# Weights, q, stores and low parts rearranged at the start of a fused attention and two-layer kernel

## The chip, the cores and the metric

The kernel runs on one core of a Trainium2 chip. The metric is the device time of one execution in microseconds (us); less is better. A core has TensorE (PE, matmuls), VectorE (DVE), ScalarE (ACT), GpSimd (POOL) and SyncE (SP), which here issues every DMA.

## The reference

Linear attention with an RMS norm, then two feed-forward layers, all in fp32:

```
kv  = einsum('bhsd,bhse->bhde', k, v)          # b=8, h=8, s=576, d=64
out = einsum('bhsd,bhde->bhse', q, kv)
out = out / sqrt(mean(out*out, -1) + 1e-6) * g_norm
x   = out, tokens x 512                        # 4608 x 512
x   = relu(x @ moe_w_in)**2 @ moe_w_out        # 512 -> 2048 -> 512
h   = x @ moe2_w_in;  x = (h * cos(h)) @ moe2_w_out
```

The layer weights arrive as 64-bit floats.

## The kernel before

A layer matmul is made of three fp32r matmuls on split operands: every fp32 value is a high part (a cast to fp32r, on ScalarE) plus a low part (a subtraction of the high part), and the product is high x high, high x low and low x high. So each weight (`wh`, `wl`), each x (`xh`, `xl`) and each activation (`gh`, `gl`) needs a cast and a subtraction before TensorE can use it.

`load_w` brings half of the weights of one f (128 of the 2048 inner columns) as raw 64-bit words, 512 KB, and `conv_w` turns them into `wh` and `wl`: five VectorE steps (L120, L122, L125, L128, L131), a ScalarE step (L121), the cast (L132) and the subtraction (L133, GpSimd). The raw tiles have two buffers; a `Stream` object loads item k+2 one chunk after item k is converted. There are 16 values of f, i = 0 is the w_in half and i = 1 the w_out half. Conversion k stands here for the k-th item: f = k // 2, i = k % 2.

The layer work is a list of chunks (stage, token tile t of 512 tokens, f). Stage 0 is the first layer with f = 0 to 7, stage 1 the same layer with f = 8 to 15, stage 2 the second layer with all 16. `layer_in` makes 12 matmuls of a chunk into a PSUM bank, `act_relu2` or `act_cos` makes `gh` and `gl`, and `layer_out` makes 12 matmuls into the accumulators, two chunks later. In stage 0, chunk n below 8 is f = n of the first token tile and needs conversion 2n for `layer_in` and 2n + 1 for `layer_out`.

Attention is cut in units (batch b, head pair group p of 4, half hf of 288 tokens). `load_kv` and `kv_mm` make K'V of a batch (five loads with five buffers), then for each unit `att_a` (matmul with q, square, scaled copy `og`), `att_b` (sum of squares by a matmul with ones, r and r2 on ScalarE), `att_c` (three VectorE operations, L251 to L253, into `xo`, and its store to `x_d`) and `att_d`, which for the first two token tiles (NDIRECT) writes `xh` and `xl` straight from `xo`. Later tiles fetch x from DRAM by `load_x` and split it by `split_x`.

Everything that isn't a chunk is a job with a position, in chunks: `at(n, fn, ...)`. Jobs run in the order of their positions between the chunks; all with n up to -1 come ahead of chunk 0. Batch 0 of the attention has its kv_mm at -13.5 and unit i at -13 + i (`att_b`, `att_c` and `att_d` at 1.5 more), batch 1 starts at -3 with steps of 0.8, and each later batch fills the eight chunks of one token tile. Weight conversions 0 to 15 stand at -5 + 0.7 k. On top of that the framework's scheduler works over the program: it orders each engine's instructions by readiness in its own plan, with the program order as priority. So an engine's order in the trace can differ from the order of positions (conversions 0 and 1 run ahead of the attention in the trace, although their positions are behind it).

The pool `att` is given back when the attention's chunks are over, and the second half of the weights is kept in its place.

Of the kernel before, what the change touches and what calls it, by code (L numbers as in the profile page):

```python
# [24 lines left out]
def kernel(  # L25
# [22 lines left out]
    NH = 8  # L48
    NW = NF // 2
    NEXACT = 2  # L50
    NQ = 4
    XH, XL = 8, 10
    S = NT // B
    HS = S // 2
# [45 lines left out]
    wpools = {0: wlo}  # L100

    def load_w(m, f, i):
        raw = conv_p.tile([P, DM, 2], U32, tag="raw", name="raw")
        nc.sync.dma_start(out=raw.rearrange("p n two -> p (n two)"), in_=(wA, wB)[m][f, :, i, :])
        raws[m, f, i] = raw

    def conv_w(m, f, i):
        raw = raws.pop((m, f, i))
        low, high = raw[:, :, 0], raw[:, :, 1]
        ahead = (m, f) in spooled  # L110
        if ahead:
            h, l = (tp.tile([P, DM], F32R, tag="t", name=f"w{x}")[:] for x in "hl")
        else:
            if i == 0:
                new_w(m, f)
            h, l = (x[:, i, :] for x in wts[m, f])
        e = tp.tile([P, DM], U32, tag="t", name="e")
        w = tp.tile([P, DM], U32, tag="t", name="w")
        ef, wf = e[:].bitcast(F32), w[:].bitcast(F32)
        nc.vector.tensor_scalar(out=e, in0=high, scalar1=0x7FF00000, scalar2=None, op0=ALU.bitwise_and)  # L120
        nc.scalar.activation(out=e[:].bitcast(I32), in_=e[:].bitcast(I32), func=AF.Relu, scale=8.0, bias=expb)  # L121
        nc.vector.tensor_scalar(  # L122
            out=w, in0=high, scalar1=12, scalar2=8, op0=ALU.logical_shift_left, op1=ALU.logical_shift_right
        )
        nc.vector.scalar_tensor_tensor(  # L125
            out=w, in0=low, scalar=28, in1=w, op0=ALU.logical_shift_right, op1=ALU.bitwise_or
        )
        nc.vector.scalar_tensor_tensor(  # L128
            out=e, in0=high, scalar=0x80000000, in1=e, op0=ALU.bitwise_and, op1=ALU.bitwise_or
        )  # L130
        nc.vector.scalar_tensor_tensor(out=wf, in0=w, scalar=float(1 << 24), in1=ef, op0=ALU.add, op1=ALU.mult)  # L131
        nc.scalar.copy(out=h, in_=wf)  # L132
        nc.gpsimd.tensor_tensor(out=l, in0=wf, in1=as32(h), op=ALU.subtract)  # L133
        if ahead:
            for k, x in enumerate((h, l)):
                nc.sync.dma_start(out=w_d[m, f][:, k, i, :], in_=as32(x))
# [77 lines left out]
    def att_a(*u):  # L214
        b, p, hf = u
        o = bank("o")[:, :HS]
        nc.tensor.matmul(o, kvs[b][:, p, :], q_sb.pop(u)[:], start=True, stop=True)  # L217
        og = att_p.tile([P, HS], F32, tag="og", name="og", bufs=4)
        sq = att_p.tile([P, HS], F32, tag="sq", name="sq", bufs=3)
        nc.scalar.activation(out=sq, in_=o, func=AF.Square)  # L220
        nc.scalar.activation(out=og, in_=o, func=AF.Copy, scale=gcol)
        if b < NEXACT:
            att[u] = (og, sq, None)
            return
        sh = att_p.tile([P, HS], F32R, tag="sh", name="sh", bufs=3)
        sl = att_p.tile([P, HS], F32R, tag="sl", name="sl", bufs=3)
        nc.scalar.copy(out=sh, in_=sq)
        nc.vector.tensor_tensor(out=sl, in0=sq, in1=as32(sh[:]), op=ALU.subtract)
        att[u] = (og, sh, sl)
# [15 lines left out]
    def att_c(*u):  # L245

        b, p, hf = u
        og, ss, r, r2 = att[u]
        m = att_p.tile([P, HS], F32, tag="m", name="m", bufs=2)
        xo = att_p.tile([P, HS], F32, tag="xo", name="xo", bufs=3)  # L250
        nc.vector.scalar_tensor_tensor(out=m, in0=ss, scalar=D * EPS, in1=r2, op0=ALU.add, op1=ALU.mult)  # L251
        nc.vector.scalar_tensor_tensor(out=m, in0=m, scalar=-3.0 * D, in1=r, op0=ALU.add, op1=ALU.mult)
        nc.vector.tensor_tensor(out=xo, in0=m, in1=og, op=ALU.mult)  # L253
        nc.sync.dma_start(out=x_d[b][:, p, hf * HS:(hf + 1) * HS], in_=xo)
        att[u] = xo

    def att_d(*u):
        b, p, hf = u
        xo = att.pop(u)
        tok = b * S + hf * HS  # L260
        for t in range(NDIRECT):
            lo, hi = max(tok, t * TOK), min(tok + HS, (t + 1) * TOK)
# [4 lines left out]
            h, l = (x[:, lo - t * TOK:hi - t * TOK] for x in xs[0, t, p])  # L267
            piece = xo[:, lo - tok:hi - tok]
            nc.scalar.copy(out=h, in_=piece)
            eng = nc.gpsimd if b == 0 else nc.vector  # L270
            eng.tensor_tensor(out=l, in0=piece, in1=as32(h), op=ALU.subtract)  # L271

    def units(b):
        return [(b, p, hf) for p in range(NKC) for hf in range(2)]
# [15 lines left out]
                n += 1  # L290
        return ps

    def act_relu2(ps, lo_eng, busy=False):
        r = tp.tile([P, TOK], F32, tag="t", name="r")
        g = tp.tile([P, TOK], F32, tag="t", name="g")
        h = g_p.tile([P, TOK], F32R, tag="gh", name="gh")
# [4 lines left out]
        else:  # L301
            nc.vector.scalar_tensor_tensor(out=g, in0=ps, scalar=0.0, in1=r, op0=ALU.max, op1=ALU.mult)
        nc.scalar.copy(out=h, in_=g)  # L303
        lo_eng.tensor_tensor(out=l, in0=g, in1=as32(h[:]), op=ALU.subtract)  # L304
        return h, l

    def act_cos(ps, lo_eng):
        k = tp.tile([P, TOK], I32, tag="t", name="k")
        y = tp.tile([P, TOK], F32, tag="t", name="y")
        h = g_p.tile([P, TOK], F32R, tag="gh", name="gh")  # L310
# [6 lines left out]
        nc.scalar.activation(out=c, in_=y, func=AF.Sin, bias=hpib)  # L317
        nc.vector.tensor_tensor(out=y, in0=ps, in1=c, op=ALU.mult)  # L318
        nc.scalar.copy(out=h, in_=y)  # L319
        lo_eng.tensor_tensor(out=l, in0=y, in1=as32(h[:]), op=ALU.subtract)  # L320
        return h, l

    def load_part(t):
# [61 lines left out]
    class Stream:  # L385
# [7 lines left out]
                self.load(*item)  # L393
            self.next += count

        def place(self, positions, after=0):
            for n, item in zip(positions, self.items):
                at(n, self.use, *item)
                at(n + after, self.advance)

    spooled = {(0, f) for f in range(NW, NF)} | {(1, f) for f in range(NH, NF)}
    conv_at = [
        (0, range(NH), -5, 0.7),
        (0, range(NH, NW), 4, 0.8),
        (0, range(NW, NF), 13, 2.6),
        (1, range(NH), nA0 + 5, 2.1),
        (1, range(NH, NF), nA0 + 5 + 2 * NH * 2.1, 2.1),
# [10 lines left out]
        w_items += [(m, f, i) for f in fs for i in range(2)]  # L418
        w_at += [n + step * k for k in range(2 * len(fs))]
    w_stream = Stream(load_w, conv_w, w_items)  # L420
    w_stream.place(w_at, 1)

    kv_stream = Stream(load_kv, kv_mm, [(b, c) for b in range(B) for c in range(NSC)])
    starts = [(-13, 1), (-3, 0.8)] + [(-3 + NH * (b - 1), NH / (2 * NKC)) for b in range(2, B)]
# [2 lines left out]
    for b, (s0, ds) in enumerate(starts):  # L427
        for i, u in enumerate(units(b)):
# [4 lines left out]
            q_items = q_items[1:]  # L433
            for fn in (att_b, att_c, att_d):
                at(n + 1.5, fn, *u)
    for st in range(3):
        f0 = NH if st == 1 else 0
        for t in range(NTILE):
            n0 = index[st, t, f0]
            for c in range(NKC):  # L440
                if st == 0 and t < NDIRECT:
                    continue
                at(n0 - 5 + c, load_x, st, t, c)
                at(n0 - 4 + c, split_x, st, t, c)
            if st == 1:
                at(n0 + 3, load_part, t)
    jobs.sort(key=lambda j: j[:2])
    done = 0

# [7 lines left out]
    def run_chunks(lo, hi, act):  # L457
        for n in range(lo, hi):
            ps = layer_in(*chunks[n])
            gs[chunks[n]] = act(ps, nc.gpsimd if n < 4 else nc.vector, *([True] if n < nAtt else []))  # L460
            run_jobs(n)
            if n >= LAG:
                layer_out(*chunks[n - LAG])
            run_jobs(n + 0.5)

    nc.vector.memset(epsb, EPS)
    nc.vector.memset(hpib, HALF_PI)
    nc.vector.memset(qrtb, 0.25)
    nc.vector.memset(expb, -float((896 + 24) << 23))
    nc.vector.memset(as32(ones[:]), 0.0)  # L470
    for j in range(2):
        nc.vector.memset(as32(ones[j * D:(j + 1) * D, j * D:(j + 1) * D]), 1.0)

    with tc.tile_pool(name="att", bufs=1) as att_p:
        kvx = [att_p.tile([P, NKC, P], F32, tag=f"kvx{b}", name=f"kvx{b}") for b in range(2)]
# [1 line left out]
            nc.gpsimd.memset(x, 0.0)  # L477
        w_stream.advance(2)
        kv_stream.advance(NSC)
        for u in units(0)[:NQ]:  # L480
            load_q(*u)
        for j in range(2):
            nc.sync.dma_start(out=gcol[j * D:(j + 1) * D, :], in_=g_norm.rearrange("(d o) -> d o", o=1))
        nc.vector.tensor_scalar(out=gcol, in0=gcol, scalar1=-0.5 / D, scalar2=None, op0=ALU.mult)
        run_jobs(-1)
        banks.update(o=["o"], ss=["ss"])
        run_chunks(0, nAtt, act_relu2)
# [48 lines left out]
```

## Time and profile before

| | us |
|---|---|
| median of 3 runs | 1717.36 (1714.54 to 1719.39) |
| profiled execution | 1713.82 |
| its span (first to last instruction) | 1712.0 |
| TensorE busy | 1677.3 (98%) |
| VectorE busy | 1000.1 (58%) |
| ScalarE busy | 774.5 (45%) |
| GpSimd busy | 245.2 (14%) |

Of the 40 equal slices of the span (42.8 us each) TensorE is busy 6, 7 and 9 tenths in the first three or nine and more in all others but the last. Busy times are sums of durations; an instruction's duration can overlap the start of the next on the same engine, and a matmul's end is modelled. Lines named L120 and so on are those of the program above. In rows, "PEld" is TensorE's weight load, "SPq" a DMA issue on SP, "<-" after the numbers names what ended the idle time before an instruction, and the granted clock of TensorE is given as a share of full speed. A row of stretches holds the stretch and its length, the busy us (and number of instructions) of PE, PEld, DVE, ACT and POOL, the granted clock, the share of the DMA engines and GB/s.

### The profile page before, as it was taken

How to read it: one execution, taken by the hardware profiler on the slowest of the kernel's cores; microseconds unless marked ns; L12 is line 12 of the kernel's file. 1: busy time of each engine (PE TensorE's matmuls, PEld its weight loads, DVE VectorE, ACT ScalarE, POOL GpSimd, SP SyncE). 2: the span in 40 equal slices, each digit the busy share in tenths (PEclk: the TensorE clock that was granted, in tenths of full speed). 3: DMA queues.
4: the chain of work that ended last, by engine and by line, in shares of the span. 5: the costliest groups of instructions: out<-in, count | busy, mean ns of one | idle time of the engine just before them, and what ended most of it. 6: DMA issues, size and time to landing. Idle time of an engine off the chain costs nothing.

```text
span 1712.0 us, 20153 instructions
## 1 busy us (share of the span) xinstructions
PE 1677.3 (98%) x7488; PEld 1381.6 (81%) x7488; DVE 1000.1 (58%) x1561; ACT 774.5 (45%) x1366; POOL 245.2 (14%) x186
## 2 busy tenths in 40 slices
PE   6799999999999999999999999999999999999998
PEld 5488888888888888878888888888888888888887
DVE  5974666566223555555555565656565656565655
ACT  5665666667333333333334343434343434343333
POOL 2321112112111222222221010101010101010000
PEclk9899999999999999999999999999999999999999
DMA  8554646544712333345457010101010101000000
GB/s 256 176 186 149 208 156 203 175 138 146 255 50 74 123 123 123 120 151 169 151 165 278 1 49 1 49 1 50 1 50 1 50 1 47 3 31 13 6 20 25
DMA packets 81571, 170.15 MB, mean 99 GB/s; under 512 B 10560, under 2 KB 38720, under 8 KB 81472
## 3 DMA queue, kind: packets, MB, share of 16 engines
q1 hardware_dynamic: 81472, 168.86, 30.3%
q8 instruction: 59, 0.97, 0.2%
q14 instruction: 40, 0.33, 0.1%
HBM read 114.30 MB, written 54.53 MB: 99 GB/s over the span
## 4 chain that ended last, share of the span: by engine, by line
PE 91%; DVE 3%; DMA 1%; issue 1%; ACT 1%; POOL 0%; SPq 0%; DVEq 0%; ACTq 0%; POOLq 0%
PE acc L343 44%; PE l L289 25%; PE ss L289 9%; PE o L289 9%; PE o L217 1%; PE o L193 1%; DVE w L125 1%; DVE e L128 1%; DVE w L131 0%; PE ss L237 0%; DMA xraw<-x_d 0%; PE ss L238 0%; DVE w L122 0%; DVE e L120 0%; DMA xraw<-y_d 0%
## 5 line engine op out<-in xcount | busy, mean ns | idle before, releaser
L289 PE MATMUL l<-xh,wh 128*128 128x512 f32 x688 | 270.8, 394 | 6.7 <-ACT r L298 4.8
L289 PE MATMUL l<-xh,wl 128*128 128x512 f32 x688 | 270.1, 393 | 2.4 <-POOL wl L133 2.4
L171 POOL TENSOR_TENSOR xl<-xraw,xh 128x512 fp32r<-128x512 f32 x100 | 141.2, 1416 | 912.9 <-ACT xh L170 890.9
L289 PE MATMUL l<-xl,wh 128*128 128x512 f32 x688 | 270.6, 393 | 0.4 <-POOL xl L271 0.4
L343 PE MATMUL acc<-gh,wh 128*128 128x512 f32 x576 | 235.4, 409 | 1.4 <-DVE ev L361 1.4
L317 ACT ACTIVATE k<-y,hpib 128x512 f32<-128x512 f32 x144 | 104.5, 725 | 283.6 <-DVE y L316 283.6
L343 PE MATMUL acc<-gh,wl 128*128 128x512 f32 x576 | 225.2, 391 | 0.0
L343 PE MATMUL acc<-wh,gh 128*128 128x512 f32 x576 | 224.2, 389 | 0.9 <-DVE ev L361 0.9
L343 PE MATMUL acc<-gl,wh 128*128 128x512 f32 x576 | 225.0, 391 | 0.0
L343 PE MATMUL acc<-wh,gl 128*128 128x512 f32 x576 | 224.1, 389 | 0.0
L343 PE MATMUL acc<-wl,gh 128*128 128x512 f32 x576 | 224.1, 389 | 0.0
L304 DVE TENSOR_TENSOR gl<-g,gh 128x512 fp32r<-128x512 f32 x140 | 99.4, 710 | 108.1 <-ACT gh L303 107.0
L320 DVE TENSOR_TENSOR gl<-y,gh 128x512 fp32r<-128x512 f32 x144 | 103.3, 717 | 97.9 <-ACT gh L319 97.8
L289 PEld LDWEIGHTS l<-xh,wh 128*128 128x128 f32 x688 | 130.0, 189 | 35.0 <-ACT r L298 6.2
L289 PEld LDWEIGHTS l<-xh,wl 128*128 128x128 f32 x688 | 130.2, 189 | 30.8 <-POOL wl L133 3.4
L289 PEld LDWEIGHTS l<-xl,wh 128*128 128x128 f32 x688 | 130.1, 189 | 26.4 <-POOL xl L271 1.2
L133 POOL TENSOR_TENSOR wl<-w,wh 128x512 fp32r<-128x512 f32 x64 | 89.7, 1402 | 349.4 <-ACT wh L132 332.8
L319 ACT CAST gh<-y 128x512 fp32r<-128x512 f32 x144 | 89.6, 622 | 105.2 <-DVE y L318 104.7
L343 PEld LDWEIGHTS acc<-gh,wh 128*128 128x128 f32 x576 | 108.3, 188 | 27.1 <-DVE ev L361 2.3
L343 PEld LDWEIGHTS acc<-gl,wh 128*128 128x128 f32 x576 | 108.3, 188 | 24.0
L343 PEld LDWEIGHTS acc<-wh,gh 128*128 128x128 f32 x576 | 108.2, 188 | 23.9 <-issue 1.2
L343 PEld LDWEIGHTS acc<-gh,wl 128*128 128x128 f32 x576 | 108.1, 188 | 22.9
(96 smaller groups left out, 2713.4 us busy)
## 6 DMA issues: line engine op xcount, KB each, us to landing
raw<-in_wA SPq DMA_DIRECT2D x32, 512.0 KB, 4.0
kvld<-in_kv SPq DMA_DIRECT2D x32, 512.0 KB, 5.7
raw<-in_wB SPq DMA_DIRECT2D x32, 512.0 KB, 4.0
q<-in_qT SPq DMA_DIRECT2D x64, 144.0 KB, 2.8
x_d<-xo SPq DMA_DIRECT2D x64, 144.0 KB, 2.1
p_d<-ev SPq DMA_DIRECT2D x18, 512.0 KB, 2.9
ev<-p_d SPq DMA_DIRECT2D x18, 512.0 KB, 5.1
y_d<-ev SPq DMA_DIRECT2D x18, 512.0 KB, 2.6
```

Of the source, the lines that this page charges most:

```text
L125: nc.vector.scalar_tensor_tensor(out=w, in0=low, scalar=28, in1=w, op0=ALU.logical_shift_right, op1=ALU.bitwise_or)
L128: nc.vector.scalar_tensor_tensor(out=e, in0=high, scalar=0x80000000, in1=e, op0=ALU.bitwise_and, op1=ALU.bitwise_or)
L133: nc.gpsimd.tensor_tensor(out=l, in0=wf, in1=as32(h), op=ALU.subtract)
L171: nc.gpsimd.tensor_tensor(out=l, in0=raw, in1=as32(h[:]), op=ALU.subtract)
L193: nc.tensor.matmul(kv_ps[b][:, p, :], t[:n, 0, p * P:(p + 1) * P], t[:n, 1, p * P:(p + 1) * P], start=(c == 0 and p == 0), stop=(c == NSC ...
L217: nc.tensor.matmul(o, kvs[b][:, p, :], q_sb.pop(u)[:], start=True, stop=True)
L289: nc.tensor.matmul(ps, a[:, 0, cs], m[:], start=(n == 0), stop=(n == 3 * NKC - 1))
L304: lo_eng.tensor_tensor(out=l, in0=g, in1=as32(h[:]), op=ALU.subtract)
L317: nc.scalar.activation(out=c, in_=y, func=AF.Sin, bias=hpib)
L319: nc.scalar.copy(out=h, in_=y)
L320: lo_eng.tensor_tensor(out=l, in0=y, in1=as32(h[:]), op=ALU.subtract)
L343: nc.tensor.matmul(o, a, m, start=(first and n == 0), stop=(last and n == 2))
```

## The change

- `NQ` goes from 4 to 8: eight loads of q (and eight buffers) ahead of the first unit, and each unit's `att_a` starts the load of the unit eight later.
- Four weight items are loaded ahead (`NRAW` = 4), the last two of them after batch 0's K and V; the items with i = 1 of f below 8 take their raw tile from the `att` pool, two more buffers. Stream items 12 and 13 load nothing, so that the lead falls back to two. Conversions 0 to 3 are placed at -14, 4 to 11 at -2.2 with steps of 0.7 (as before for the first of them), 12 to 15 at 4 with steps of 0.8.
- The store of `xo` becomes its own job, `att_e`, 0.8 chunk after `att_c`.
- Low parts move from GpSimd to VectorE: `wl` of the first 16 conversions, `xl` of batch 0 in `att_d`, and `gl` of chunks 0 to 3.
- `sh` and `sl` have two buffers instead of three.
- `load_x` and `split_x` come half a chunk later; `load_part` stays.
- The load of `g_norm` and its scaling come first in the program, and an `Abs_reciprocal_sqrt` that writes a constant's tile before the constant is set.

```diff
--- before.py
+++ after.py
@@ -48,7 +48,8 @@
     NH = 8
     NW = NF // 2
     NEXACT = 2
-    NQ = 4
+    NQ = 8
+    NRAW = 4
     XH, XL = 8, 10
     S = NT // B
     HS = S // 2
@@ -100,7 +101,8 @@
     wpools = {0: wlo}
 
     def load_w(m, f, i):
-        raw = conv_p.tile([P, DM, 2], U32, tag="raw", name="raw")
+        pool = att_p if (m, i) == (0, 1) and f < NW else conv_p
+        raw = pool.tile([P, DM, 2], U32, tag="raw", name="raw", bufs=2)
         nc.sync.dma_start(out=raw.rearrange("p n two -> p (n two)"), in_=(wA, wB)[m][f, :, i, :])
         raws[m, f, i] = raw
 
@@ -130,7 +132,7 @@
         )
         nc.vector.scalar_tensor_tensor(out=wf, in0=w, scalar=float(1 << 24), in1=ef, op0=ALU.add, op1=ALU.mult)
         nc.scalar.copy(out=h, in_=wf)
-        nc.gpsimd.tensor_tensor(out=l, in0=wf, in1=as32(h), op=ALU.subtract)
+        (nc.gpsimd if ahead or m else nc.vector).tensor_tensor(out=l, in0=wf, in1=as32(h), op=ALU.subtract)
         if ahead:
             for k, x in enumerate((h, l)):
                 nc.sync.dma_start(out=w_d[m, f][:, k, i, :], in_=as32(x))
@@ -222,8 +224,8 @@
         if b < NEXACT:
             att[u] = (og, sq, None)
             return
-        sh = att_p.tile([P, HS], F32R, tag="sh", name="sh", bufs=3)
-        sl = att_p.tile([P, HS], F32R, tag="sl", name="sl", bufs=3)
+        sh = att_p.tile([P, HS], F32R, tag="sh", name="sh", bufs=2)
+        sl = att_p.tile([P, HS], F32R, tag="sl", name="sl", bufs=2)
         nc.scalar.copy(out=sh, in_=sq)
         nc.vector.tensor_tensor(out=sl, in0=sq, in1=as32(sh[:]), op=ALU.subtract)
         att[u] = (og, sh, sl)
@@ -251,12 +253,11 @@
         nc.vector.scalar_tensor_tensor(out=m, in0=ss, scalar=D * EPS, in1=r2, op0=ALU.add, op1=ALU.mult)
         nc.vector.scalar_tensor_tensor(out=m, in0=m, scalar=-3.0 * D, in1=r, op0=ALU.add, op1=ALU.mult)
         nc.vector.tensor_tensor(out=xo, in0=m, in1=og, op=ALU.mult)
-        nc.sync.dma_start(out=x_d[b][:, p, hf * HS:(hf + 1) * HS], in_=xo)
         att[u] = xo
 
     def att_d(*u):
         b, p, hf = u
-        xo = att.pop(u)
+        xo = att[u]
         tok = b * S + hf * HS
         for t in range(NDIRECT):
             lo, hi = max(tok, t * TOK), min(tok + HS, (t + 1) * TOK)
@@ -267,8 +268,11 @@
             h, l = (x[:, lo - t * TOK:hi - t * TOK] for x in xs[0, t, p])
             piece = xo[:, lo - tok:hi - tok]
             nc.scalar.copy(out=h, in_=piece)
-            eng = nc.gpsimd if b == 0 else nc.vector
-            eng.tensor_tensor(out=l, in0=piece, in1=as32(h), op=ALU.subtract)
+            nc.vector.tensor_tensor(out=l, in0=piece, in1=as32(h), op=ALU.subtract)
+
+    def att_e(*u):
+        b, p, hf = u
+        nc.sync.dma_start(out=x_d[b][:, p, hf * HS:(hf + 1) * HS], in_=att.pop(u))
 
     def units(b):
         return [(b, p, hf) for p in range(NKC) for hf in range(2)]
@@ -290,7 +294,7 @@
                 n += 1
         return ps
 
-    def act_relu2(ps, lo_eng, busy=False):
+    def act_relu2(ps, busy=False):
         r = tp.tile([P, TOK], F32, tag="t", name="r")
         g = tp.tile([P, TOK], F32, tag="t", name="g")
         h = g_p.tile([P, TOK], F32R, tag="gh", name="gh")
@@ -301,10 +305,10 @@
         else:
             nc.vector.scalar_tensor_tensor(out=g, in0=ps, scalar=0.0, in1=r, op0=ALU.max, op1=ALU.mult)
         nc.scalar.copy(out=h, in_=g)
-        lo_eng.tensor_tensor(out=l, in0=g, in1=as32(h[:]), op=ALU.subtract)
+        nc.vector.tensor_tensor(out=l, in0=g, in1=as32(h[:]), op=ALU.subtract)
         return h, l
 
-    def act_cos(ps, lo_eng):
+    def act_cos(ps):
         k = tp.tile([P, TOK], I32, tag="t", name="k")
         y = tp.tile([P, TOK], F32, tag="t", name="y")
         h = g_p.tile([P, TOK], F32R, tag="gh", name="gh")
@@ -317,7 +321,7 @@
         nc.scalar.activation(out=c, in_=y, func=AF.Sin, bias=hpib)
         nc.vector.tensor_tensor(out=y, in0=ps, in1=c, op=ALU.mult)
         nc.scalar.copy(out=h, in_=y)
-        lo_eng.tensor_tensor(out=l, in0=y, in1=as32(h[:]), op=ALU.subtract)
+        nc.vector.tensor_tensor(out=l, in0=y, in1=as32(h[:]), op=ALU.subtract)
         return h, l
 
     def load_part(t):
@@ -393,15 +397,17 @@
                 self.load(*item)
             self.next += count
 
-        def place(self, positions, after=0):
-            for n, item in zip(positions, self.items):
+        def place(self, positions, after=0, skip=()):
+            for k, (n, item) in enumerate(zip(positions, self.items)):
                 at(n, self.use, *item)
-                at(n + after, self.advance)
+                if k not in skip:
+                    at(n + after, self.advance)
 
     spooled = {(0, f) for f in range(NW, NF)} | {(1, f) for f in range(NH, NF)}
     conv_at = [
-        (0, range(NH), -5, 0.7),
-        (0, range(NH, NW), 4, 0.8),
+        (0, range(2), -14, 0.1),
+        (0, range(2, 6), -2.2, 0.7),
+        (0, range(6, NW), 4, 0.8),
         (0, range(NW, NF), 13, 2.6),
         (1, range(NH), nA0 + 5, 2.1),
         (1, range(NH, NF), nA0 + 5 + 2 * NH * 2.1, 2.1),
@@ -418,7 +424,7 @@
         w_items += [(m, f, i) for f in fs for i in range(2)]
         w_at += [n + step * k for k in range(2 * len(fs))]
     w_stream = Stream(load_w, conv_w, w_items)
-    w_stream.place(w_at, 1)
+    w_stream.place(w_at, 1, range(2 * NW - NRAW, 2 * NW - NRAW + 2))
 
     kv_stream = Stream(load_kv, kv_mm, [(b, c) for b in range(B) for c in range(NSC)])
     starts = [(-13, 1), (-3, 0.8)] + [(-3 + NH * (b - 1), NH / (2 * NKC)) for b in range(2, B)]
@@ -433,17 +439,18 @@
             q_items = q_items[1:]
             for fn in (att_b, att_c, att_d):
                 at(n + 1.5, fn, *u)
+            at(n + 2.3, att_e, *u)
     for st in range(3):
         f0 = NH if st == 1 else 0
         for t in range(NTILE):
-            n0 = index[st, t, f0]
+            n0 = index[st, t, f0] + 0.5
             for c in range(NKC):
                 if st == 0 and t < NDIRECT:
                     continue
                 at(n0 - 5 + c, load_x, st, t, c)
                 at(n0 - 4 + c, split_x, st, t, c)
             if st == 1:
-                at(n0 + 3, load_part, t)
+                at(n0 + 2.5, load_part, t)
     jobs.sort(key=lambda j: j[:2])
     done = 0
 
@@ -457,19 +464,23 @@
     def run_chunks(lo, hi, act):
         for n in range(lo, hi):
             ps = layer_in(*chunks[n])
-            gs[chunks[n]] = act(ps, nc.gpsimd if n < 4 else nc.vector, *([True] if n < nAtt else []))
+            gs[chunks[n]] = act(ps, *([True] if n < nAtt else []))
             run_jobs(n)
             if n >= LAG:
                 layer_out(*chunks[n - LAG])
             run_jobs(n + 0.5)
 
+    for j in range(2):
+        nc.sync.dma_start(out=gcol[j * D:(j + 1) * D, :], in_=g_norm.rearrange("(d o) -> d o", o=1))
     nc.vector.memset(epsb, EPS)
+    nc.scalar.activation(out=hpib, in_=epsb, func=AF.Abs_reciprocal_sqrt)
     nc.vector.memset(hpib, HALF_PI)
     nc.vector.memset(qrtb, 0.25)
     nc.vector.memset(expb, -float((896 + 24) << 23))
     nc.vector.memset(as32(ones[:]), 0.0)
     for j in range(2):
         nc.vector.memset(as32(ones[j * D:(j + 1) * D, j * D:(j + 1) * D]), 1.0)
+    nc.vector.tensor_scalar(out=gcol, in0=gcol, scalar1=-0.5 / D, scalar2=None, op0=ALU.mult)
 
     with tc.tile_pool(name="att", bufs=1) as att_p:
         kvx = [att_p.tile([P, NKC, P], F32, tag=f"kvx{b}", name=f"kvx{b}") for b in range(2)]
@@ -477,11 +488,9 @@
             nc.gpsimd.memset(x, 0.0)
         w_stream.advance(2)
         kv_stream.advance(NSC)
+        w_stream.advance(NRAW - 2)
         for u in units(0)[:NQ]:
             load_q(*u)
-        for j in range(2):
-            nc.sync.dma_start(out=gcol[j * D:(j + 1) * D, :], in_=g_norm.rearrange("(d o) -> d o", o=1))
-        nc.vector.tensor_scalar(out=gcol, in0=gcol, scalar1=-0.5 / D, scalar2=None, op0=ALU.mult)
         run_jobs(-1)
         banks.update(o=["o"], ss=["ss"])
         run_chunks(0, nAtt, act_relu2)
```

## Rows read from the trace of the kernel before

**Rows 1.** Stretches of the span: length, busy time of each engine, granted clock, DMA.

```profile
16.15:49.60 33.45, 27.08 (x111) 18.83 (x111) 18.69 (x36) 24.41 (x63) 9.53 (x13) 0.90 0.82 248
...
49.60:105.87 56.27, 45.48 (x184) 34.41 (x185) 55.26 (x89) 36.15 (x75) 23.81 (x15) 0.85 0.57 180
...
105.87:1712.00 1606.13, 1598.06 (x7154) 1322.21 (x7154) 920.21 (x1419) 709.24 (x1223) 208.18 (x150) 1.00 0.28 92
```

**Rows 2.** Timeline of TensorE at chunk 7's layer-in: start, duration, instruction, idle before.

```profile
107.24 0.50 PE L289 MATMUL l<-xh,wl 128*128 128x512 f32 x1 [0.63 <-POOL wl L133]
```

**Rows 3.** Chain of waits, 49.6 to 105.9 us, shares by line.

```profile
by line: DVE w L125 18.2%; DVE w L131 13.9%; DVE e L128 11.8%; issue 11.1%; DVE w L122 9.6%; DMA kvld<-in_kv 7.7%; DVE xo L253 6.4%; DVE e L120 4.9%; PE o L217 2.4%; POOL wl L133 2.3%; DVE xl L271 2.3%; ACT e L121 2.2%; ACT wh L132 2.0%; DV
```

**Rows 4.** VectorE's groups, 49.6 to 105.2 us: busy us, mean ns, idle before.

```profile
L125 DVE SCALAR_TENSOR_TENSOR w<-raw,w 128x512 uint32<-128x512 uint32 x12 | 14.2, 1185 | 0.0
...
L131 DVE SCALAR_TENSOR_TENSOR w<-w,e 128x512 f32<-128x512 uint32 x12 | 10.2, 849 | 0.0
...
L128 DVE SCALAR_TENSOR_TENSOR e<-raw,e 128x512 uint32<-128x512 uint32 x12 | 9.9, 829 | 0.3 <-ACT e L121 0.3
...
L122 DVE TENSOR_SCALAR w<-raw 128x512 uint32<-128x512 uint32 x12 | 7.2, 599 | 0.0
...
L120 DVE TENSOR_SCALAR e<-raw 128x512 uint32<-128x512 uint32 x12 | 6.1, 507 | 0.0
...
L253 DVE TENSOR_TENSOR xo<-m,og 128x288 f32<-128x288 f32 x7 | 4.2, 602 | 0.5 <-DVE m L252 0.5
```

**Rows 5.** The same view, 0 to 16 us.

```profile
L120 DVE TENSOR_SCALAR e<-raw 128x512 uint32<-128x512 uint32 x2 | 0.8, 424 | 3.3 <-DMA raw<-in_wA 3.3
```

**Rows 6.** Timeline of GpSimd and VectorE, 57 to 79 us.

```profile
57.86 1.38 POOL L133 TENSOR_TENSOR wl<-w,wh 128x512 fp32r<-128x512 f32 x1 [2.31 <-ACT wh L132]
...
58.03 1.75 DVE L125 SCALAR_TENSOR_TENSOR w<-raw,w 128x512 uint32<-128x512 uint32 x1
...
77.49 0.68 DVE L125 SCALAR_TENSOR_TENSOR w<-raw,w 128x512 uint32<-128x512 uint32 x1
...
78.09 0.68 DVE L128 SCALAR_TENSOR_TENSOR e<-raw,e 128x512 uint32<-128x512 uint32 x1
```

**Rows 7.** GpSimd's groups, 49.6 to 105.2 us.

```profile
L133 POOL TENSOR_TENSOR wl<-w,wh 128x512 fp32r<-128x512 f32 x11 | 18.4, 1668 | 30.6 <-ACT wh L132 30.6
...
L304 POOL TENSOR_TENSOR gl<-g,gh 128x512 fp32r<-128x512 f32 x4 | 5.6, 1392 | 5.3 <-ACT gh L303 2.6 <-issue 2.6
```

**Rows 8.** VectorE's groups, 16 to 49.6 us.

```profile
L253 DVE TENSOR_TENSOR xo<-m,og 128x288 f32<-128x288 f32 x10 | 6.2, 621 | 1.0 <-DVE m L252 0.5
...
L252 DVE SCALAR_TENSOR_TENSOR m<-m,r 128x288 f32<-128x288 f32 x10 | 5.6, 565 | 0.3
...
L251 DVE SCALAR_TENSOR_TENSOR m<-ss,r 128x288 f32<-128x288 f32 x6 | 2.7, 454 | 12.6 <-ACT r L242 12.6
```

**Rows 9.** Loads of q issued at 4.51 and 16.91: size, us to landing.

```profile
q<-in_qT SPq DMA_DIRECT2D x1, 144.0 KB, 9.7
...
q<-in_qT SPq DMA_DIRECT2D x1, 144.0 KB, 6.2
```

**Rows 10.** Timeline of all engines, 4 to 22 us.

```profile
4.51 3.43 SPq L211 DMA_DIRECT2D q<-in_qT  x4
...
18.61 1.28 ACT L240 ACT_TABLE_LOAD   x1
...
19.91 0.50 ACT L240 ACTIVATE r<-ss,epsb 128x288 f32<-128x288 f32 x1
...
21.07 0.46 DVE L251 SCALAR_TENSOR_TENSOR m<-ss,r 128x288 f32<-128x288 f32 x1 [5.04 <-ACT r L242]
```

**Rows 11.** Stretch of 6 to 10 us, columns as in rows 1.

```profile
6.00:10.00 4.00, 2.37 (x11) 2.37 (x12) 3.97 (x8) 1.22 (x2) 0.00 (x0) 1.00 1.02 418
```

**Rows 12.** Timeline at a tile's start in stage 2, GpSimd and TensorE.

```profile
1095.85 3.05 POOL L171 TENSOR_TENSOR xl<-xraw,xh 128x512 fp32r<-128x512 f32 x2 [3.14 <-ACT xh L170]
...
1099.65 0.39 PE L289 MATMUL l<-xl,wh 128*128 128x512 f32 x1
```

## The prediction

> **What bounds the kernel now.** I read the page first: TensorE's slices are full but for the first few, so I cut the span at the places where it changes. From 105.87 us to the end TensorE is idle 8.1 us in 1606, at full clock; in the two stretches before, 16.15 to 49.6 and 49.6 to 105.87, it is idle 6.4 and 10.8 us and its granted clock is 0.90 and 0.85 [rows 1]. Only the start can be shortened. My mark is the first layer-in of chunk 7 (the last f of the first token tile): it begins at 105.87 us, and its third matmul, which needs the low part of a weight, at 107.24 after a wait for GpSimd [rows 2]. From there TensorE is full whatever came earlier, so what the mark gains, the kernel gains.
>
> What holds the mark? The chain of waits over 49.6 to 105.9 runs mainly through VectorE's five steps of the weight conversion (L120, L122, L125, L128, L131) [rows 3]. VectorE is busy 55.26 of 56.27 us there, TensorE 45.48, ScalarE 36.15 [rows 1]. VectorE is the limit: fifteen conversions (0 to 14, two for each f) must be done before chunk 7 starts.
>
> But it isn't working all that time. L125 takes a mean of 1185 ns in this stretch, L131 849, L128 829, L122 599, L120 507, L253 602 [rows 4]. Undisturbed, L120 and L122 take 424 and about the same [rows 5], and the three others 0.68, L253 some 0.45 [rows 6, 8]. The long ones are those that meet GpSimd: its low part of a weight starts at 57.86 for 1.38 us, and the L125 that starts at 58.03 takes 1.75 us and ends 0.54 us after GpSimd [rows 6]. Count by (mean less undisturbed) the excess is 6.0 + 2.0 + 1.8 + 2.1 + 1.0 + 1.1 = 14.0 us, beside fifteen GpSimd instructions (11 of L133, 4 of L304) [rows 7]: a little under 1 us each.
>
> **Stretch B (49.6 to the mark).** The edit puts those fifteen on VectorE and leaves GpSimd nothing else there. Removed: 14.0 us of stall. Added: from start to start one 512-wide two-input operation costs VectorE 0.60 us when the next follows [rows 6]. One wl of the eleven leaves with conversion 3, which is now made ahead of the attention, so ten wl and four gl: 14 x 0.60 = 8.4. Conversion 3's own steps take off 2 x 0.34 + 3 x 0.60 = 2.5 (0.34 is 0.42 less the same overlap of 0.08). Sum -14.0 + 8.4 - 2.5 = -8.1 us. At the mark the last wl, 1.3 us on GpSimd, becomes 0.68 on VectorE: -0.6. TensorE could be the next limit, but its 45.5 busy us, part of them at a low clock, and ScalarE's 36 stay below the 56.3 - 8.1 = 48.2 left.
>
> **Stretch A (16.15 to 49.6), gains.** Conversion 2 moves ahead: -2.5. Batch 0's low parts come to VectorE: four units of 288 columns, and four cut in 224 and 64. From 0.45 less 0.08 for 288 columns [rows 8] I estimate 0.37, 0.30 and 0.15 by width: 4 x 0.82 = +3.3. In exchange L253 (621 ns, ten) and L252 (565, ten) fall to 450 [rows 8]: -2.9. VectorE waits 12.6 us before L251, for ScalarE [rows 8], of which 5.0 is the start before 21.07 [rows 10], so 7.6 are pauses. The larger ones have causes that the change touches. The fifth load of q stood behind the next batch's K and V and landed after 6.2 us [rows 9], so that layer matmuls were put in front of its unit; with eight q ahead, units 4 to 7 follow directly. And where batch 1 starts, conversions whose weights are now there can fill. I count 5 of the 7.6 as won; bounds 0 and 7.6.
>
> The early dummy rsqrt takes a table load of 1.28 us out of the first unit; the next activation starts 0.02 us after it [rows 10]. The Trainium skill (ScalarE: Activation LUTs, What ACT_TABLE_LOAD costs) puts a switch at about 2.66 us, with a drain of 1.38; no drain shows in this row, and by that figure the sum would be up to 1.4 us better.
>
> **Stretch A, costs.** The DMA engines are full at 6 to 10 us, with 418 GB/s [rows 11]. The two tiny loads of gcol now come first; SP took 0.86 us for each issue of q with its waits [rows 10], I estimate half, 0.8 for both. Two more weight tiles, 1.05 MB, stand ahead of q: 2.5 us at that rate. The first q, issued at 4.51, landed after 9.7, at 14.2 [rows 9, 10]; now 17.5. The first unit's matmul would be at 17.5 instead of 16.15, and from it to the first L251 it was 4.9 us, less the table load 3.6: 21.1, as before. But conversions 2 and 3 are on VectorE then: raw 2 lands about 16.2 (14.2 + 0.8 and one tile, 1.25, more), and two conversions with wl take 2 x 3.1 us: 22.3. Cost +1.2 us (bounds 0, and 2.9 if the queue is a further 1.7 late).
>
> The stores of x move behind one more unit, and behind what the loads put in the queue: the last q lands at 17.5 + 7 x 0.35 = 20, then 4.5 tiles of K and V and four weight tiles, 10.6 us, so the first store lands after 30. xo has three buffers: unit 3's L253, due near 22.3 + 3 x 1.7 + 1 = 28.4 (1.7 a unit: three operations of 0.45 and a low part of 0.37), would wait, and behind it on VectorE every conversion and low part, and behind those chunk 0. Conversions ordered in front of it would hide that. I take +2; bounds 0 and 5.
>
> Sum A: -2.5 + 3.3 - 2.9 - 5 + 1.2 + 2 = -3.9.
>
> **Costed at nothing.** sh and sl lose a buffer: they live 1.5 chunks in units a chunk apart, and TensorE reads the old pair before it makes what fills the new; with that cover gone, ScalarE would wait for one matmul narrower than that of 0.39 us in [rows 12]. The half chunk's delay of x's loads and splits is hidden by the slack under rival 3. Conversions 12 to 15 are placed 0.6 to 0.9 chunk later and again served two ahead; chunk 7's weight still has a chunk of time.
>
> **Sum.** -8.1 - 0.6 - 3.9 = -12.6 us. The profiled execution took 1713.82 us (span 1712.0), inside the spread of the three runs, whose median is 1717.36; taken from the median: 1704.8 (profiled like before: 1701.2).
>
> **Rivals.** (1) The front gives it back. With no pause won, a store wait of 5 and a start 2.9 later, A is -2.5 + 3.3 - 2.9 + 0 + 2.9 + 5 = +5.8, the sum -2.9: 1714.5, no change to be measured. For it: what is issued later lands later here, a q after 9.7 us behind K, V and weights [rows 9]. The Trainium skill (DMA: Bandwidth & Descriptors, Two DMAs through the same engine are not ordered) says that descriptors of one queue start in order; the landing times agree. Against it: VectorE has conversions to fill such waits. 0.13.
> (2) The long VectorE rows come not from GpSimd but, say, from transfers into SBUF. Then the added 8.4 + 3.3 stay and 14.0 + 2.9 don't go: -12.6 + 16.9 = +4.3, 1721.7. [Rows 6] speak against it. 0.04, half of it counted slower.
> (3) Late splits, on the other side. At a tile's start late in the kernel GpSimd's last two low parts of x end at 1098.90, and the matmul that needs the last starts at 1099.65 [rows 12]: 0.75 us of slack. If the half chunk (some 2.9 us: 1606 us after the mark hold 281 chunks) goes through to the split, TensorE waits 2.1 us at each of 25 tile starts: +53, net 1758. It decides from 12.6 / 25 = 0.5 us a tile. Against it: between the old and the new place ScalarE and GpSimd have no other work in those stages, so their order stays. 0.05.
>
> **Chances.** The forecast has 0.78, the rivals 0.13, 0.04 and 0.05. About 0.3% (5.2 us) can be told from nothing here. Best end: all pauses won, no store wait, no late start: -12.6 - 2.6 - 2 - 1.2 = -18.4, 1699. The upper end takes in rival 1: 1715. The forecast alone: 1699 to 1711. Outside the range: rivals 2 and 3 and the forecast's own misses. Faster 0.80 (with a little of rival 1), same 0.13, slower 0.07.
>
> **What would show it.** After: L125 near 0.69 us everywhere before the mark, GpSimd without wl and gl there; chunk 7's first matmul at 90 to 97 us; no table load in the attention; first L251 near 22; under 5 us of pauses on VectorE after it; TensorE as full after the mark as before. Wrong would be: VectorE waiting for x's stores, TensorE waiting for xl at tile starts, or a mark later than 101.

## The result and the profile after

The changed kernel takes 1701.11 us (median of 4 runs, 1699.40 to 1702.52), the kernel before, run beside it, 1715.95 us (4 runs, 1714.22 to 1719.39): ratio 0.9911, interval 0.9891 to 0.9930, or 14.8 us less. The forecast was 12.6 less. The profiled execution took 1699.40 us with a span of 1697.6, so 14.4 less span than before. The steps of the conversion are now L122, L124, L127, L130, L133 and its low part L135; `att_c` is L253 to L255, its split L270 and L271, `gl` L308, the layer-in L293 and the layer-out L347.

Windows of the changed kernel, columns as in [rows 1], with chunk 7's new start, 96 us, in place of the old 105.87:

```profile
16.15:49.60 33.45, 25.73 (x112) 19.10 (x111) 27.89 (x64) 25.07 (x65) 0.00 (x0) 0.90 0.84 279
...
49.60:96.00 46.40, 45.42 (x214) 36.10 (x213) 44.89 (x97) 39.56 (x87) 0.00 (x0) 1.00 0.76 253
...
96.00:1697.60 1601.60, 1592.19 (x7133) 1319.07 (x7131) 919.40 (x1415) 702.18 (x1209) 204.47 (x148) 1.00 0.28 90
```

GpSimd has no instruction in either early stretch, where it had 9.53 and 23.81 us [rows 1]. In the middle one VectorE is busy 44.89 of 46.40 us, and TensorE too, 45.42, at full clock and no longer at 0.85. After it TensorE is idle 9.4 us in 1602, much as before (8.1 in 1606).

Timeline of TensorE where chunk 7 starts, to set beside [rows 2]:

```profile
94.34 0.61 PE L347 MATMUL acc<-gh,wh 128*128 128x512 f32 x1
...
95.02 0.41 PE L293 MATMUL l<-xh,wh 128*128 128x512 f32 x1
...
95.96 0.39 PE L293 MATMUL l<-xh,wl 128*128 128x512 f32 x1
```

The first matmul with a low part of the weight comes at 95.96 us instead of 107.24, 11.3 earlier, and waits for nothing. That is less than the 14.4 by which the span fell, because the order on TensorE changed. The groups of one kind of layer-out matmul, from 30 us to each kernel's mark, before:

```profile
L343 PE MATMUL acc<-gh,wh 128*128 128x512 f32 x20 | 8.6, 430 | 0.0
```

and after:

```profile
L347 PE MATMUL acc<-gh,wh 128*128 128x512 f32 x25 | 10.9, 435 | 0.0
```

All three kinds together count 60 before (chunks 0 to 4) and 74 after: chunk 5's twelve and two of chunk 6 are done already, whereas before they came after the mark. From start to start such a matmul takes some 0.23 us, so 14 of them are 3.2 us, and 11.3 + 3.2 = 14.5 us, about what the span gained. (Smaller items nearly cancel: four more matmuls ahead of this point, two of layer-in and two with q, are some 0.9 us more, and TensorE is idle 1.3 us more after it.) So the gain is made by 96 us and kept.

VectorE's groups of the changed kernel, 49.6 to 96 us, columns as in [rows 4]:

```profile
L127 DVE SCALAR_TENSOR_TENSOR w<-raw,w 128x512 uint32<-128x512 uint32 x10 | 6.9, 689 | 0.0
L130 DVE SCALAR_TENSOR_TENSOR e<-raw,e 128x512 uint32<-128x512 uint32 x10 | 6.9, 689 | 0.0
L133 DVE SCALAR_TENSOR_TENSOR w<-w,e 128x512 f32<-128x512 uint32 x10 | 6.9, 689 | 0.0
L135 DVE TENSOR_TENSOR wl<-w,wh 128x512 fp32r<-128x512 f32 x9 | 6.2, 692 | 0.8 <-ACT wh L134 0.7
L308 DVE TENSOR_TENSOR gl<-g,gh 128x512 fp32r<-128x512 f32 x7 | 4.8, 691 | 0.0
L124 DVE TENSOR_SCALAR w<-raw 128x512 uint32<-128x512 uint32 x10 | 4.3, 425 | 0.0
...
L255 DVE TENSOR_TENSOR xo<-m,og 128x288 f32<-128x288 f32 x7 | 3.2, 459 | 0.0
```

The same operations that took means of 1185, 829, 849 and 602 ns [rows 4] now take 689, 689, 689 and 459 ns (L127, L130, L133 and L255); L124 (before L122, 599) takes 425.

The first stretch went less smoothly. Timeline of VectorE, changed kernel, the starts that matter:

```profile
16.67 0.43 DVE L122 TENSOR_SCALAR e<-raw 128x512 uint32<-128x512 uint32 x1 [3.23 <-DMA raw<-in_wA]
...
24.35 0.46 DVE L253 SCALAR_TENSOR_TENSOR m<-ss,r 128x288 f32<-128x288 f32 x1 [1.38 <-ACT r L244]
...
30.35 0.46 DVE L254 SCALAR_TENSOR_TENSOR m<-m,r 128x288 f32<-128x288 f32 x1
...
40.67 0.45 DVE L255 TENSOR_TENSOR xo<-m,og 128x288 f32<-128x288 f32 x1
```

Two things stand here. The attention's first VectorE step starts at 24.35 us, not near 22. And the fourth unit's L254 runs at 30.35, but its L255, which writes the fourth `xo` into three buffers, only at 40.67; conversions 4 and 5 run between. Why the start is late stands in ScalarE's timeline:

```profile
19.53 0.72 ACT L123 ACTIVATE e<-e,expb 128x512 int32<-128x512 int32 x1 [1.09 <-DVE e L122]
20.16 0.60 ACT L134 CAST wh<-w 128x512 fp32r<-128x512 f32 x1
20.79 0.41 ACT L222 ACTIVATE sq<-acc 128x288 f32<-128x288 f32 x1
```

ScalarE's own steps of conversions 2 and 3 stand in front of the first square, which thus starts at 20.79 although its matmul started at 18.48. And the store that frees the first `xo`, in the transfers issued from 29 to 29.7 us (size, us to landing):

```profile
x_d<-xo SPq DMA_DIRECT2D x1, 144.0 KB, 6.7
```

It is issued at 29.30 and lands at 36.0, behind the weight tiles and q in the queue; one issued at 41.15 lands after 1.8 us.

### The profile page after: what moved, and what is told of

Its sections match the earlier page's. It is cut to its first block, busy times and chain, and to the rows that moved or that the text cites. A ratio compares the mean times of both kernels' runs of the same rounds, so it can differ in the third digit from the quotient of the medians.

```text
span 1697.6 us, 20188 instructions
## 1 busy us (share of the span) xinstructions
PE 1670.1 (98%) x7488; PEld 1380.8 (81%) x7488; DVE 999.4 (59%) x1593; ACT 770.9 (45%) x1366; POOL 205.7 (12%) x154
## 4 chain that ended last, share of the span: by engine, by line
PE 94%; DVE 2%; DMA 1%; ACT 1%; issue 1%; SPq 0%; POOL 0%; DVEq 0%; ACTq 0%; POOLq 0%
PE acc L347 45%; PE l L293 26%; PE ss L293 9%; PE o L293 9%; PE o L195 2%; PE o L219 1%; DMA kvld<-in_kv 1%; DMA xraw<-x_d 0%; PE ss L239 0%; PE ss L240 0%; DVE e L130 0%; DMA xraw<-y_d 0%; PE ss L237 0%; DVE e L122 0%; DVE ev L365 0%
## 5 line engine op out<-in xcount | busy, mean ns | idle before, releaser
L293 PE MATMUL l<-xh,wh 128*128 128x512 f32 x688 | 269.4, 392 | 3.5 <-ACT xh L270 2.5
L293 PE MATMUL l<-xl,wh 128*128 128x512 f32 x688 | 270.4, 393 | 0.0
L293 PE MATMUL l<-xh,wl 128*128 128x512 f32 x688 | 268.6, 390 | 0.0
L347 PE MATMUL acc<-gh,wh 128*128 128x512 f32 x576 | 235.5, 409 | 2.4 <-DVE ev L365 2.3
L347 PE MATMUL acc<-wh,gh 128*128 128x512 f32 x576 | 224.6, 390 | 2.0 <-DVE ev L365 2.0
L347 PE MATMUL acc<-gh,wl 128*128 128x512 f32 x576 | 226.0, 392 | 0.0
L347 PE MATMUL acc<-gl,wh 128*128 128x512 f32 x576 | 225.5, 391 | 0.0
L347 PE MATMUL acc<-wl,gh 128*128 128x512 f32 x576 | 224.4, 390 | 0.0
L347 PE MATMUL acc<-wh,gl 128*128 128x512 f32 x576 | 224.3, 389 | 0.0
L308 DVE TENSOR_TENSOR gl<-g,gh 128x512 fp32r<-128x512 f32 x144 | 102.9, 715 | 105.2 <-ACT gh L307 104.2
L293 PEld LDWEIGHTS l<-xh,wh 128*128 128x128 f32 x688 | 129.3, 188 | 30.5 <-ACT xh L270 3.1
L293 PEld LDWEIGHTS l<-xh,wl 128*128 128x128 f32 x688 | 129.5, 188 | 27.3 <-DVE wl L135 0.2
L293 PEld LDWEIGHTS l<-xl,wh 128*128 128x128 f32 x688 | 129.5, 188 | 25.2
L347 PEld LDWEIGHTS acc<-gh,wh 128*128 128x128 f32 x576 | 108.3, 188 | 27.9 <-DVE ev L365 2.1
L347 PEld LDWEIGHTS acc<-wh,gh 128*128 128x128 f32 x576 | 108.3, 188 | 24.9 <-issue 2.4
L347 PEld LDWEIGHTS acc<-gl,wh 128*128 128x128 f32 x576 | 108.3, 188 | 23.9
L347 PEld LDWEIGHTS acc<-gh,wl 128*128 128x128 f32 x576 | 108.1, 188 | 22.6
L347 PEld LDWEIGHTS acc<-wh,gl 128*128 128x128 f32 x576 | 108.2, 188 | 22.4
```

The costliest lines, as they stand in the source:

```text
L293: nc.tensor.matmul(ps, a[:, 0, cs], m[:], start=(n == 0), stop=(n == 3 * NKC - 1))
L308: nc.vector.tensor_tensor(out=l, in0=g, in1=as32(h[:]), op=ALU.subtract)
L347: nc.tensor.matmul(o, a, m, start=(first and n == 0), stop=(last and n == 2))
```

## The experiments

Each ratio is to the kernel before, run beside it (median 1716.55 us for the first four experiments, 1717.75 for the next four, 1718.15 for the last four). Differences to the changed kernel across these groups are rough. My theory: two parts that add up, GpSimd off VectorE's path and earlier work from earlier loads. The rivals: only one of them counts, or the long VectorE rows don't come from GpSimd.

**The low parts alone** (the kernel before, three lines):

```diff
-        nc.gpsimd.tensor_tensor(out=l, in0=wf, in1=as32(h), op=ALU.subtract)
+        (nc.gpsimd if ahead or m else nc.vector).tensor_tensor(out=l, in0=wf, in1=as32(h), op=ALU.subtract)
-            eng = nc.gpsimd if b == 0 else nc.vector
+            eng = nc.vector
-            gs[chunks[n]] = act(ps, nc.gpsimd if n < 4 else nc.vector, *([True] if n < nAtt else []))
+            gs[chunks[n]] = act(ps, nc.vector, *([True] if n < nAtt else []))
```

> The kernel before with the low parts of the first 16 conversions, of batch 0's x and of the first four chunks on VectorE, and nothing else. If VectorE's long rows are waits for GpSimd: 14.0 + 2.9 us of them go, 15 x 0.60 + 3.3 us of work come, 0.6 at the last wl: about -5 us (-3 to -7), 1711 against 1716, and L125 near 0.69 us in 50 to 105 us. If they come from something else: the added 12 us of work stay, about 1728, and L125 stays above 1.1 us.

1709.23 us, 0.9953 (0.9938 to 0.9968): -7.3 us. Group of VectorE, 49.6 to 105.2 us:

```profile
L125 DVE SCALAR_TENSOR_TENSOR w<-raw,w 128x512 uint32<-128x512 uint32 x12 | 8.2, 682 | 0.0
```

The very line that took 1185 ns [rows 4] takes 682 with GpSimd empty and the loads as they were.

**The loads alone** (the kernel before with `NQ` 8, `NRAW` 4, the new places of the conversions, the second `raw` pool and two buffers of `sh` and `sl`; GpSimd keeps the low parts, and the stores stay early).

> The kernel before with four weight loads and eight loads of q ahead, the conversions' new places and the buffers for them; low parts, stores, x loads and the start as before. If pauses and two conversions leave the bound stretch: about -6 us (-2 to -9), 1710. If the front gives it back (late q, the loads' traffic): 0 to +2, 1716 to 1718.

1709.42 us, 0.9954 (0.9940 to 0.9969): -7.1 us. The two alone make -14.4, the whole change -14.8: within the intervals they add. The whole holds more pieces, though (the late stores, the reordered start, x's half chunk). With the low parts undone (next) they stand on top of the loads, and the gain is -7.7, as for the loads alone: there those pieces together cost or gave nothing that can be told.

**The low parts back on GpSimd** (the changed kernel with those three places undone).

> The changed kernel with all the moved low parts back on GpSimd. If GpSimd's instructions hold VectorE up: 5 to 8 us slower than the changed kernel, 1706 to 1709, and L127 well above 0.69 us in 50 to 100 us. If the gain is the loads' alone: 1701.

1708.87 us, 0.9955 (0.9941 to 0.9968), 7.8 above the changed kernel. The conversion's step on VectorE, 49.6 to 96 us, is long again:

```profile
L127 DVE SCALAR_TENSOR_TENSOR w<-raw,w 128x512 uint32<-128x512 uint32 x9 | 7.7, 855 | 0.0
```

**GpSimd busy for nothing** (the changed kernel; after the low part of conversions 4 to 15, GpSimd makes the same subtraction once more into a buffer that nobody reads):

```diff
+        if (m, f) in early:
+            nc.gpsimd.tensor_tensor(out=ef, in0=wf, in1=as32(h), op=ALU.subtract)
```

> The changed kernel, with one more GpSimd subtraction of 128x512 for each of conversions 4 to 15, whose result nobody reads; VectorE has exactly the work of the changed kernel. If the two engines shut each other out: about 12 x 1 us = +12 (8 to 14), 1711 to 1715, with the conversion's VectorE steps lengthened by some 12 us in all. If VectorE's long rows had another cause (traffic into SBUF, say): no change, 1701.

1707.15 us, 0.9946 (0.9932 to 0.9960): 6 us above the changed kernel. So mere GpSimd work makes the kernel slower, but half as much as I expected. Groups of the two low parts, VectorE's needed one and GpSimd's unread one, 30 to 96 us:

```profile
L135 DVE TENSOR_TENSOR wl<-w,wh 128x512 fp32r<-128x512 f32 x9 | 9.4, 1047 | 0.7 <-ACT wh L134 0.7
...
L137 POOL TENSOR_TENSOR e<-w,wh 128x512 f32<-128x512 f32 x9 | 22.8, 2535 | 74.1 <-ACT wh L134 74.1
```

In this stretch the lines of VectorE that grew (L135 from 692 ns to 1047; also L127, L130, L133, L257 and a split) grew by 7.5 us for these nine, 0.8 each, near the 14.0 / 15 = 0.93 of the kernel before. At the mark most of the expected cost is there: chunk 7's layer-in starts at 104.60 us instead of 95.02, 9.6 later, with 74 layer-out matmuls ahead of it in both. Ten of the twelve extra instructions start before it (nine by 96 us), two after it. Behind the mark some of that comes back: TensorE is idle 7.1 us there, in the changed kernel 9.4; the span grew by 7.4. One part of the 9.6 isn't lengthening: the extra instruction also keeps a buffer of `e`, and VectorE waits for it once, 1.18 us, at 98.71. And GpSimd waits too: its mean is 2535 ns. Timeline of GpSimd:

```profile
57.96 3.30 POOL L137 TENSOR_TENSOR e<-w,wh 128x512 f32<-128x512 f32 x1 [14.82 <-ACT wh L134]
62.61 1.32 POOL L137 TENSOR_TENSOR e<-w,wh 128x512 f32<-128x512 f32 x1 [1.35 <-ACT wh L134]
```

and of VectorE in the same kernel:

```profile
59.43 0.69 DVE L130 SCALAR_TENSOR_TENSOR e<-raw,e 128x512 uint32<-128x512 uint32 x1
60.03 0.45 DVE L255 SCALAR_TENSOR_TENSOR m<-ss,r 128x288 f32<-128x288 f32 x1
60.40 1.41 DVE L133 SCALAR_TENSOR_TENSOR w<-w,e 128x512 f32<-128x512 uint32 x1
...
62.71 1.78 DVE L135 TENSOR_TENSOR wl<-w,wh 128x512 fp32r<-128x512 f32 x1
...
70.00 1.40 DVE L273 TENSOR_TENSOR xl<-xo,xh 128x160 fp32r<-128x160 f32 x1
```

The second GpSimd row starts before L135 and takes 1.32 us, and L135 waits until it ends. The first takes 3.30 and ends at 61.26; less 1.32 it got in at 59.94, as VectorE came to L255 at 60.03, which reads its `ss` from PSUM and is not lengthened. The L133 behind it is. A later one, of 2.42 us from 68.80, got in by the same sum at 69.90, beside an L124, which has one input; the L273 at 70.00 is the one lengthened, from 0.32 to 1.40. So whoever has begun goes on, and the other stands still. The Trainium skill (SBUF — State Buffer, SBUF: two separate sides) says this: GpSimd and a VectorE operation with two SBUF inputs share a pair of ports, and the one that starts first holds it for its whole instruction. The trace agrees, in these rows and in [rows 6].

**What the late stores cost: four buffers of `xo`, and the stores back behind `att_c`** (each alone on the changed kernel):

```diff
-        xo = att_p.tile([P, HS], F32, tag="xo", name="xo", bufs=3)
+        xo = att_p.tile([P, HS], F32, tag="xo", name="xo", bufs=4)
```

> The changed kernel with four buffers for xo instead of three. In the changed kernel unit 3's L255 runs at 40.67 us, some 10 us after what it needs, behind two conversions; the store that frees its buffer lands at 36.0. If that wait costs the kernel: batch 0 ends earlier than 49 us and the time falls by 1 to 4 us, 1697 to 1700. If VectorE's sum of work is what counts and the conversions fill the wait: within 1 us of 1701.

```diff
         nc.vector.tensor_tensor(out=xo, in0=m, in1=og, op=ALU.mult)
+        nc.sync.dma_start(out=x_d[b][:, p, hf * HS:(hf + 1) * HS], in_=xo)
```

> The changed kernel with the store of xo back behind L255. If the late place of the stores is what holds batch 0 up: first store issued near 27 instead of 29.3, unit 3 earlier, 1 to 3 us faster, 1698 to 1700. If the stores then make SP wait with loads behind them, as before: 1 to 4 us slower, 1702 to 1705. If VectorE's sum decides: 1701.

Four buffers: 1696.70 us, 0.9876 (0.9862 to 0.9889), some 5 us below the changed kernel. Early stores: 1698.67, 0.9887 (0.9874 to 0.9901), some 3 below, at the edge of what can be told. With four buffers the fourth unit's L255 runs in its turn; timeline of VectorE there:

```profile
31.11 0.45 DVE L255 TENSOR_TENSOR xo<-m,og 128x288 f32<-128x288 f32 x1
```

The next unit's then waits until 40.00: the hole moved by one unit and didn't close. With early stores it isn't closed either. SP issues the first store at 28.67, not near 27, it lands after 8.2 us, at 36.9, and the fourth unit still comes late; timeline of VectorE in that run:

```profile
39.36 0.45 DVE L255 TENSOR_TENSOR xo<-m,og 128x288 f32<-128x288 f32 x1
```

So the buffer, not the place of the store, sets which unit waits. What the wait costs in whole no run shows, and the 3 us of the early stores, if they are real, don't come from an earlier landing of the first store.

**The start: the two extra weight loads behind the eight q, and the start's small loads and the dummy rsqrt undone.**

```diff
-        w_stream.advance(NRAW - 2)
         for u in units(0)[:NQ]:
             load_q(*u)
+        w_stream.advance(NRAW - 2)
```

> The changed kernel with the two extra weight loads behind the eight q instead of in front. First unit's matmul near 16.5 instead of 18.48 us and first L253 near 21.5 instead of 24.35, but conversions 2 and 3 some 3 us later. If a late q costs the kernel: 1 to 3 us faster, 1698 to 1700. If VectorE must simply always have work: its idle 3.2 us before conversion 2 moves elsewhere, within 1 us of 1701.

```diff
-    nc.scalar.activation(out=hpib, in_=epsb, func=AF.Abs_reciprocal_sqrt)
```

> The changed kernel with the loads of g_norm and their scaling behind the loads of q again, and without the early rsqrt, so that a table load of 1.28 us stands in the first unit again. Loads land about 1.4 us earlier, the first unit pays 1.28: within 1.5 us of 1701. If a switch of tables cost 2.66 us: some 1 to 2 us slower; if gcol's place in front costs more than the table load: 1 to 2 faster.

1700.21 us, 0.9903 (0.9886 to 0.9920), and 1700.75, 0.9898 (0.9884 to 0.9911): both as the changed kernel. With q first the attention's first L253 starts three microseconds earlier, but VectorE has had nothing to do ahead of it, and nothing comes of it; timeline of VectorE:

```profile
21.29 0.46 DVE L253 SCALAR_TENSOR_TENSOR m<-ss,r 128x288 f32<-128x288 f32 x1 [7.78 <-ACT r L244]
```

Without the dummy the table load is back in the first unit; timeline of ScalarE:

```profile
20.04 1.28 ACT L242 ACT_TABLE_LOAD   x1
21.33 0.50 ACT L242 ACTIVATE r<-ss,epsb 128x288 f32<-128x288 f32 x1
```

It takes 1.28 us, and the time isn't longer. But the same run has its loads earlier: conversion 2 starts at 15.22 us instead of 16.67, and the first L253 at 22.34 instead of 24.35. The run shows the two edits together to be worth nothing, not either by itself.

**Put together, with the changed kernel as a control.**

> The changed kernel once more, beside the three below on one chip, to compare them with: 0.991 of the kernel before.

> The changed kernel with four buffers for xo and the store back behind L255. If both edits cure the same wait (unit 3's xo for the store of unit 0), they don't add: as four buffers alone, 0.9875 to 0.989 of before. If the stores' place costs something of its own: the sum, 0.985.

> The changed kernel with four buffers for xo and the two extra weight loads behind the eight q. If an earlier first unit is worth something once the wait for xo is gone: 1 to 3 us less than four buffers alone, 0.986 to 0.987 of before. If VectorE's work decides: 0.9875.

> The changed kernel with four buffers for xo and the loads in this order: one weight tile, K and V, four q, three weight tiles, four q. TensorE's first matmul near 8 instead of 9.2 us and the first unit some 3 us earlier, but VectorE has only one conversion to do meanwhile instead of two. If TensorE's and ScalarE's early start counts: 2 us less than four buffers alone, 0.986. If VectorE must have work early: 2 to 3 us more, 0.989.

The changed kernel again: 1701.04 us, 0.9905 (0.9891 to 0.9918). Four buffers with early stores: **1693.90 us, 0.9863 (0.9849 to 0.9876)**, 7 us below the changed kernel, the lowest of all, though its interval meets that of four buffers alone. Four buffers with q first: 1700.83, 0.9903 (0.9887 to 0.9919). Four buffers with the queue in the order one weight tile, K and V, four q, three weight tiles, four q: 1700.60, 0.9904 (0.9889 to 0.9918). In these two the gain of the fourth buffer is gone, which none of my alternatives had. Windows from the start to 49.6 and on to 90 us, changed kernel:

```profile
0.00:49.60 49.60, 32.47 (x145) 25.66 (x146) 35.13 (x84) 29.12 (x71) 1.19 (x6) 0.93 0.83 274
49.60:90.00 40.40, 39.42 (x188) 31.53 (x187) 38.90 (x85) 34.00 (x75) 0.00 (x0) 1.00 0.82 274
```

four buffers and early stores:

```profile
0.00:49.60 49.60, 34.66 (x156) 25.50 (x156) 36.77 (x89) 31.99 (x80) 1.19 (x6) 0.93 0.83 277
49.60:90.00 40.40, 40.40 (x196) 33.39 (x195) 39.18 (x84) 33.36 (x73) 0.00 (x0) 1.00 0.86 274
```

four buffers and q first:

```profile
0.00:49.60 49.60, 32.62 (x143) 24.32 (x143) 32.87 (x81) 28.46 (x72) 1.19 (x6) 0.93 0.80 266
```

and the low parts alone:

```profile
49.60:90.00 40.40, 33.32 (x149) 26.69 (x150) 37.73 (x79) 28.54 (x58) 0.00 (x0) 0.92 0.60 192
```

With low parts and loads both changed, TensorE is nearly full from 49.6 us on, so what is left to win lies ahead of it. The best version has TensorE busy 2.2 us longer and VectorE 1.6 us longer by 49.6, and TensorE idle not at all from there to 90. With four buffers and q first TensorE is about where the changed kernel has it, and VectorE 2.3 us below. VectorE waits 7.46 us for its first L253 there and later 0.74 and 1.53 us for casts of ScalarE; its waits from 13.5 to 49.6 us sum to 10.2 us, with four buffers alone to 5.7.

## Why the prediction was right

**The bound and the mark: right, with a reading to mend.** The gain was made before chunk 7, whose first matmul came at 95.02 (forecast 90 to 97). But its start alone shows 11 of the 14.4 us; layer-out matmuls had moved from behind the mark to ahead of it. TensorE, which I had put below the limit at 45.5 of 48.2 us, is as full as VectorE after the change (45.42 and 44.89 of 46.40), for it does this extra work in a shorter stretch. That it could is in part luck. At the mean of the stretch before, 45.48 / 184 = 0.247 us, its 214 matmuls would take 52.9 us (an estimate; the mix of matmuls differs a little), more than the 46.4 there are. The granted clock rose from 0.85 to 1.00 with the fuller stretch, and my sum had no term for it.

**The low parts: mechanism shown, a little undersized.** My terms for them by themselves were -14.0 for the stalls, +9.0 for fifteen operations (fourteen in the whole change, where conversion 3 moves ahead), -0.6 at the mark, +3.3 and -2.9 in the first stretch: -5.2. Measured were -7.3 alone and -7.8 on top of the loads. The prices by piece hold: 689 ns for one operation, 0.8 us of stall for an extra GpSimd subtraction.

**The loads: right in sum.** Conversions 2 and 3 (-5.0), pauses won (-5), start (+1.2) and store wait (+2) made -6.8. The run that has all of these, the low parts back on GpSimd, is 7.7 below the kernel before. The loads by themselves, without late stores and so without the +2, were -7.1 against -8.8. The intervals don't tell more.

**The start: mis-sized, and no cost.** I took 22.3 us for the first L253, from VectorE's share of conversions 2 and 3; it was 24.35, since ScalarE's share stood in front of the squares. But starting at 21.29 gained nothing where VectorE waited 7.78 us for it, so the +1.2 isn't shown: what VectorE did meanwhile, two conversions, was needed anyway. The 1.28 us of the table load no run prices by itself.

**The store wait: right place, too small.** +2 with a bound of 5 stood for the fourth unit's wait, and it came at that unit. A fourth buffer, which only moves the wait to the fifth unit, is worth some 5 us, with early stores 7; the whole cost of the wait wasn't measured. Conversions filled the hole, as I said, but only two of them, each with a wait for ScalarE of up to 0.7 us, and VectorE came back to the unit 4.7 us after the store had landed.

**The pauses.** After 24.35 VectorE pauses some 2.7 us to 49.6, under the 5 forecast.

**The rivals.** The front didn't give the gain back, though its store wait is there. That the long rows have another cause than GpSimd is refuted by the first and the fourth experiment. TensorE waits for no split of x after 96 us; its waits there are these (total us, times, longest):

```profile
PE acc L347 <- DVE ev L365: 4.3, 3, 2.0
```

**What stays open.** Why the fourth buffer's gain vanishes when q comes earlier. The planner orders each engine's queue anew for each version, so one place in the program changes much else; VectorE waits longer and has less work done by 49.6 us, but no run changes that alone. For the same reason the gain of the fourth buffer itself isn't shown to be the wait for the store and nothing else. The half chunk by which x's loads were moved was not tried by itself.

## What to carry to other kernels

Where VectorE is the limit, don't count work on GpSimd as free: price one GpSimd instruction by what the neighbouring VectorE rows exceed their undisturbed duration, and compare that with doing it on VectorE (here 0.8 to 0.9 us against 0.60). When stores move behind prefetched loads of one queue, count buffers against the landing time, not the issue. And a mark on one engine measures a gain only if the same work lies ahead of it in both traces: count the instructions.

## What the hardware showed that I had not expected

- GpSimd is held up as well: an unread 128x512 subtraction took 2.54 us on average beside a full VectorE against 1.32 us undisturbed. Of its long rows, two got in where a VectorE instruction read PSUM (3.30 and 3.80 us) and one beside an instruction with one input (2.42).
- The mean granted clock of TensorE in the middle stretch was 0.85 before, when it was busy 45.48 of 56.27 us, and 1.00 after, busy 45.42 of 46.40.
- A 144 KB store took 6.7 us to land when loads had been issued ahead of it, and 1.8 us twelve microseconds later, with the DMA engines idle before it.
- A table load takes 1.28 us and the next activation starts 0.01 us after it; no drain shows in that row or the next.
